# The sum of a unit's logits issued one place later on VectorE, in a delta-rule attention and mixture-of-experts kernel

## The chip, the cores and the metric

One core of a Trainium2 chip runs the whole program. The metric is the device time of one execution in microseconds, from three runs of the kernel; the profile is one further execution, with its own time.

## The reference

Four sequences of 768 tokens with eight heads of 48 features go through a delta rule; the 3072 rows of 384 that come out of it go through a layer of eight experts, each row to the one expert with the largest logit.

```python
k_n = k / (np.linalg.norm(k, axis=-1, keepdims=True) + 1e-06)
for t in range(S):
    y[:, :, t] = q_t @ state
    state = state + beta_t * outer(k_t, v_t - state @ k_t)
...
logits = x @ w_gate
expert_idx = np.argmax(logits, axis=1)
gate_w = softmax(logits)[expert_idx]
out[mask_e] = gate_w * (np.maximum(x[mask_e] @ w1[e], 0.0) @ w2[e])
```

## The kernel before

The work has two parts on one time line. The first part is attention: the 768 tokens are cut into six blocks of 128, and a **unit** n is one block of one of the four sequences (24 units). A main loop runs steps t = 0 to 26. In step t, TensorE computes `residual(t)` (products of states and earlier results, into the tile `ks`, lines L424 and L436), VectorE subtracts them from the values (`v_all`, L443), TensorE applies the inverse of a small triangular system (`apply`, L451, which reads `v_all`), and ScalarE copies the result to `u` (L455). The output of a unit follows three steps behind (`finish`): products of its query with the state (`yp`, L474), an update of the state (`ku`, L483, added on VectorE at L487), products with `u` (again `yp`, L492), two ScalarE copies to `yt` (L496). One step later `emit_x` multiplies `yt` with a selection matrix `esel` that also holds the gate's weights: four products (`xp`, L516) give the unit's 384 features and, in four pieces, its eight logits. ScalarE copies the features to `row` (L517), and VectorE sums the pieces of the logits to `rl` (TENSOR_REDUCE, L518).

The inverses of later blocks are computed on VectorE alone, as long chains of small operations on `lw`, `lg` and `tmp` (L384, L388). Nothing schedules them but the code: `beside(t, i)`, at seven places i of each step, issues a share of them (`inverses`), then a few pieces of the routing of finished rows (the list `fine`), and near the end shares of the second part. All engines work in the order of issue (a manual schedule), so the order of these calls is the order on each engine.

Routing of a pair of units (`pool_slots`, units 0 to 15) starts with a maximum on VectorE (`mx`, L617) and goes on with some twenty small operations on GpSimd (POOL in the rows): a mask of the chosen expert `oh_all` (L620 to L635), a count by four tiny products on TensorE (`pp`, L639 and L642), a ScalarE copy (`ct`, L645), positions (L647 to L654), the row numbers `sli` (L660), and two indirect DMAs that scatter the pair's rows to the experts' table `xg` in DRAM (L666). Each `yield` in these generators is a point where `beside` may go on with something else. For the later units `emit_slots` does the same on VectorE (L534 to L582, products at L552 and L555, scatters at L589); the last four units go through it one at a time. When the rows of units 16 and 17 have been scattered, `load_main` loads the first 256 rows of expert 0 (`xr`, L731), and TensorE transposes them (`xt`, L784), to begin with expert 0 while attention still runs (`early`, steps 23 to 26: first layer tiles h_0 to h_7 at L759, relu on ScalarE and VectorE at L762 and L763, weights split in two at L694 and L695).

Short PSUM tiles come from a ring of three buffers with the tag "y": `yp`, `ku`, `xp` and `pp` take them in the order of issue, and each waits until the last reader of the tile three places before it is done. GpSimd also copies a block's norms (`nt_all`, L339, four copies) when VectorE has transposed them (`r`, L334), masks the query products (`pm`, L277), and clears `lw` (L283).

The second part, from 302 us on, is the eight experts' layers on TensorE (`ffn`, products at L759 and L770).

Of the kernel before, what the change touches and what calls it, by code (L numbers as in the profile page):

```python
# [41 lines left out]
def deltanet_moe(ctx, tc, kt_d, qt_d, kn_d, v_d, beta_d, w_gate, w1, w2, out):  # L42
# [402 lines left out]
    def apply(t):  # L445

        ks, vn = tiles["ks", t], vt[t]
        for h in range(H):
            for q, n in stage(t):
                r = slice(32 * q, 32 * q + 32)  # L450
                nc.tensor.matmul(ks[r, h, :], lhsT=tiles[n // B]["wt"][r, n % B * H + h, :], rhs=vn[r, h, :],  # L451
                                 start=True, stop=True, tile_position=(32 * q, 32 * q), skip_group_check=True)
        for i, (q, n) in enumerate(reversed(stage(t))):
            r = slice(32 * q, 32 * q + 32)
            nc.scalar.copy(out=uview(n)[r], in_=ks[r])  # L455
            if i == 2:
                yield

    def finish(n):

        tb, b = n // B, n % B
        last = tb == NT - 1
        st, u = st_t[b], uview(n)
        qt, pm = qt_t[n % QTL], pm_t[n % QSL]
        yp = [pss.tile([128, NP // 2, C], F32, name=f"yp{tb}_{b}_0", tag="y", bufs=YB),
              psg_[-1].tile([128, NP // 2, C], F32, name=f"yp{tb}_{b}_1", tag="g")]

        def place(h, m):
            o = 64 * ((h // 2 + h) % 2)
            return yp[h // 2 % 2][o:o + m, h // 4, :]  # L470

        for h in range(H):
            r = slice(64 * (h % 2), 64 * (h % 2) + 64)
            nc.tensor.matmul(place(h, 64), lhsT=st[r, h // 2, r], rhs=qt[r, h // 2, :], start=(h < 4), stop=True,  # L474
                             tile_position=(r.start, 64 * ((h // 2 + h) % 2)), skip_group_check=True)
        yield
        if not last:
            ku = pss.tile([112, NP, D], F32, name=f"ku{tb}_{b}", tag="y", bufs=YB)
            for h in range(H):

                m = 64 if h % 2 == 0 else D
                kn = tiles[tb][b]["kn"].rearrange("t h d -> t (h d)")[:, h * D:h * D + m]
                nc.tensor.matmul(ku[64 * (h % 2):64 * (h % 2) + m, h // 2, :], lhsT=kn, rhs=u[:, h, :],  # L483
                                 start=True, stop=True, skip_group_check=True)
            for a in range(2):
                r = slice(64 * a, 64 * a + D)
                nc.vector.tensor_tensor(out=st[r, :, r], in0=st[r, :, r], in1=ku[r], op=ALU.add)  # L487
            if n + NB_ < NN - B:
                load_ku(n + NB_)
        yield  # L490
        for h in range(H):
            nc.tensor.matmul(place(h, D), lhsT=u[:, h, :], rhs=pm[:, h, :],  # L492
                             start=False, stop=True, skip_group_check=True)
        yt = lp.tile([128, NP, C], F32, name=f"yt{tb}_{b}", tag="yt", bufs=2)
        for o in range(2):
            nc.scalar.copy(out=yt[:, o::2], in_=yp[o])  # L496
        yield
        w = 1 if n >= NN - W1 else 2
        if n % w == 0:
            tiles["row", n // w, w] = (rp if n < NN - 2 else xq_[0]).tile([128, 2 if n < NN - 2 else 1, ROW], F32, name=f"row{tb}_{b}", tag="row", bufs=2)  # L500
            tiles["rl", n // w, w] = lp.tile([128, 2, E], F32, name=f"rl{tb}_{b}", tag="rl", bufs=2)
        row, rl = tiles["row", n // w, w], tiles["rl", n // w, w]
        row, rl = row[:, 0:w], rl[:, 0:w]
        emit_x(n, yt, row[:, n % w], rl[:, n % w])
        if n % w == w - 1:
            fine.append((pool_slots if n < PG else emit_slots)(tb, b - w + 1, w, row, rl))

# [1 line left out]
        t = st_t[b][:, p, :]  # L509
        return bass.AP(tensor=t.tensor, offset=t.offset, ap=[list(t.ap[0]), [64, 2], [1, D]])  # L510

    def emit_x(n, yt, row, rl):

        xp = pss.tile([128, NP, 2 * D + E], F32, name=f"xp{n // B}_{n % B}", tag="y", bufs=YB)
        for p in range(NP):
            nc.tensor.matmul(xp[:, p, :], lhsT=yt[:, p, :], rhs=esel[:, p, :], start=True, stop=True)  # L516
        nc.scalar.copy(out=row[:, 0:DM].rearrange("t (p c) -> t p c", p=NP), in_=xp[:, :, 0:2 * D])  # L517
        nc.vector.tensor_reduce(out=rl, in_=xp[:, :, 2 * D:].rearrange("t p e -> t e p"), axis=AX.X, op=ALU.add)  # L518

    def emit_slots(tb, b, w, row, rl):  # L520

# [454 lines left out]
    def beside(t, i):  # L976

        place[0] = 7 * t + i
        for tb in ROOT:
            if place[0] == ROOT[tb][0]:  # L980
                squares(tb)
            if place[0] == ROOT[tb][1]:
                root(tb)
        inverses((SPEND0 if t < B else SPEND if t < 3 * B else SPEND2)[i], t)
        for _ in range(STEPS[i] if t < NN - B else 4):
            if fine and not run(fine[0]):
                fine.pop(0)
        for _ in range(WSL.count((t, i))):
            run(W)
        for _ in range(ES.count((t, i))):  # L990
            ahead_step()

    fin = iter(())
    for t in range(NN + LAG):
        if t < NN and t % B == 0 and t > 0:
            while line and line[0].tb <= t // B:
                inverse_step(t)
            if t == NN - B:
                ep_.close()
                wq.append(ep.enter_context(tc.tile_pool(name="wr", bufs=1, side="right")))  # L1000
                xq_.append(ep.enter_context(tc.tile_pool(name="xq", bufs=1, side="right")))
                W = pieces()
                run(W)
        residual(t)
        beside(t, 0)
        chunk(ks_, t)
        run(fin)
        if t + 1 < NN + LAG and not B <= t < NN - B:
            scale_v(t + 1)
        if t + 1 < NN:  # L1010
            clear_u(t + 1)
        beside(t, 1)
        copies = apply(t)
        run(copies)
        for tb in range(1, NT):
            for i in range(NB):
                if t == B * (tb - 1) + i:
                    load_v(tb, i)
        fin = finish(t - LAG) if t >= LAG else iter(())
        run(fin)  # L1020
        beside(t, 2)
        run(fin)
        run(copies)

        if B <= t < NN - B:
            scale_v(t + 1, act=True)
        beside(t, 3)
        beside(t, 4)
        run(fin)
        beside(t, 5)  # L1030
        chunk(qs_, t)
        beside(t, 6)
        if t >= LAG:
            load_k(t - LAG + KTL)
            load_q(t - LAG + QTL)
        for x in slots[CL[t]:CL[t + 1]] if t + 1 < len(CL) else ():
            nc.sync.dma_start(out=x, in_=zrow[0:x.shape[0]].unsqueeze(1).broadcast_to(x.shape))
    i = 0
    run(fin)
    while fine:  # L1040
        if not run(fine[0]):
            fine.pop(0)
# [304 lines left out]
```

## Time and profile before

| | |
|---|---|
| median of 3 runs | 526.48 us (524.97 to 529.17) |
| profiled execution, its own time | 525.89 us |
| its span, first to last instruction | 524.2 us |
| TensorE, VectorE, ScalarE, GpSimd busy in the span | 463.6, 331.6, 269.5, 142.9 us |
| granted TensorE clock, mean | 0.955 |

Every number in a row of the trace is of the one profiled execution. Its time of 525.89 us is 1.7 us more than its span. A bracket at the end of a timeline row, such as [2.00 <-ACT row L517], is the time that the engine stood idle before that instruction, and what ended it. PE is TensorE's products, DVE is VectorE, ACT is ScalarE, POOL is GpSimd, SP issues most DMAs.

### The profile page before, as it was taken

Reading aid. Unit: us, or ns where it says so; the run is one execution under the profiler, and the core shown is the slowest. Engines: PE = TensorE matmul, PEld = TensorE weight load, DVE = VectorE, ACT = ScalarE, POOL = GpSimd, SP = SyncE. Lnnn points to the kernel's source line nnn. Section 1 sums busy time; section 2 is a strip of 40 time slices with the busy share of each in tenths; the row PEclk is TensorE's granted clock in tenths of the full one; section 3 lists DMA queues with packets and bytes.
Section 4 is the critical chain, followed back from the end, with each engine's and each line's share of the span. In section 5 each row is a group of like instructions: output and inputs, shape, how many; then the busy total and the mean of one; then the engine's idle time right before and its main releaser. Section 6 shows DMA issues by size and latency. Waiting matters only on the chain. (4 is left out here: it accounts for less than half of the span.)

```text
span 524.2 us, 17557 instructions
## 1 busy us (share of the span) xinstructions
PE 463.6 (88%) x7212; PEld 426.7 (81%) x7212; DVE 331.6 (63%) x996; ACT 269.5 (51%) x622; POOL 142.9 (27%) x305
## 2 busy tenths in 40 slices
PE   6866769899888888988789999999999999999995
PEld 4755658788776767777689889999999999999995
DVE  3989999698897689435654386636372827445330
ACT  2542236588676667755644246535354636354320
POOL 7002011465763655433130201020202020110202
PEclk9976689899999899898999999999999999999998
DMA  5878769569479557394442156555373636453001
GB/s 165 194 256 227 232 153 315 168 157 294 119 198 275 183 159 225 123 301 123 151 157 80 67 158 221 177 168 160 123 226 114 211 129 210 137 163 108 33 3 44
DMA packets 66060, 87.88 MB, mean 168 GB/s; under 512 B 26425, under 2 KB 50767, under 8 KB 65968
## 3 DMA queue, kind: packets, MB, share of 16 engines
q1 hardware_dynamic: 62512, 77.01, 50.2%
q0 software_dynamic: 3456, 9.57, 5.0%
q8 instruction: 67, 1.10, 0.9%
q14 instruction: 25, 0.20, 0.1%
HBM read 60.24 MB, written 23.56 MB: 160 GB/s over the span
## 5 line engine op out<-in xcount | busy, mean ns | idle before, releaser
L770 PE MATMUL y<-w2h,hx 128*128 128x384 f32 x352 | 93.8, 341 | 0.4 <-PEq L1143 0.4
L773 POOL DMA_INDIRECT out_dram<-yo,idx x32 | 30.7, 958 | 202.3 <-ACT yo L1116 129.8
L695 DVE TENSOR_TENSOR w2l<-w2r,w2h 128x768 fp32r<-128x768 f32 x32 | 31.2, 978 | 69.9 <-ACT w2h L694 69.7
L388 DVE TENSOR_TENSOR lw<-lw,tmp 128x84 f32<-128x84 f32 (+29 forms) x239 | 67.3, 316 | 0.4
L384 DVE TENSOR_TENSOR tmp<-lg,lw 128x84 f32<-128x84 f32 (+29 forms) x239 | 65.2, 307 | 2.5
L770 PEld LDWEIGHTS y<-w2h,hx 128*128 128x128 f32 x352 | 64.1, 188 | 0.7 <-issue 0.7
L455 ACT COPY u<-ks 32x384 f32<-32x384 f32 x96 | 45.1, 470 | 32.8 <-PE ks L451 30.3
L770 PE MATMUL y<-w2l,hx 128*128 128x384 f32 x176 | 59.4, 337 | 0.0
L759 PE MATMUL h<-xl,w1h 128*128 128x384 f32 (+1 forms) x168 | 57.5, 342 | 0.2 <-DVE xl L695 0.2
L759 PE MATMUL h<-xh,w1h 128*128 128x384 f32 (+1 forms) x168 | 57.5, 342 | 0.0
L759 PE MATMUL h<-xh,w1l 128*128 128x384 f32 (+1 forms) x168 | 57.4, 342 | 0.0
L762 ACT ACTIVATE hx<-h 128x448 fp32r<-128x448 f32 (+1 forms) x64 | 32.9, 518 | 33.1 <-PE h L759 32.3
L424 PE MATMUL ks<-st,kt 128*32 128x96 f32 x768 | 46.2, 257 | 2.4 <-issue 2.4
L1116 ACT ACTIVATE yo<-y,gt 128x384 f32<-128x384 f32 x21 | 12.2, 582 | 66.9 <-PE y L770 51.0
L763 DVE SCALAR_TENSOR_TENSOR hx<-h,hx 128x448 fp32r<-128x448 f32 (+1 forms) x64 | 36.9, 587 | 15.1 <-ACT hx L762 14.9
L277 POOL TENSOR_SCALAR_AFFINE_SELECT pm<-pm 128x1024 f32<-128x1024 f32 x24 | 26.6, 1110 | 71.2 <-ACT pm L276 68.6
L451 PE MATMUL ks<-v_all,wt 32*32 32x48 f32 x1536 | 25.7, 206 | 21.6 <-DVE v_all L443 18.9
L249 ACT COPY gg<-pg 128x512 f32<-128x512 f32 x48 | 25.8, 588 | 35.2 <-PE pg L266 35.2
L451 PEld LDWEIGHTS ks<-v_all,wt 32*32 32x32 f32 x1536 | 21.5, 107 | 26.0 <-DVE v_all L443 21.7
L424 PEld LDWEIGHTS ks<-st,kt 128*32 128x32 f32 x768 | 34.5, 113 | 5.8 <-issue 2.9
L266 PE MATMUL pq<-qt,kt 64*128 64x128 f32 x384 | 32.1, 299 | 2.3 <-issue 1.0
L695 DVE TENSOR_TENSOR w1l<-w1r,w1h 128x1024 fp32r<-128x1024 f32 x24 | 29.4, 1225 | 6.8 <-ACT w1h L694 6.8
(194 smaller groups left out, 987.9 us busy)
## 6 DMA issues: line engine op xcount, KB each, us to landing
w1r<-in_w_dram SPq DMA_DIRECT2D x24, 512.0 KB, 4.0
w2r<-in_w_dram SPq DMA_DIRECT2D x32, 384.0 KB, 3.7
kt<-in_kt_dram SPq DMA_DIRECT2D x24, 256.0 KB, 2.8
qt<-in_qt_dram SPq DMA_DIRECT2D x24, 256.0 KB, 5.8
xg<-zrow SPq DMA_DIRECT2D x7, 788.0 KB, 6.2
kg<-in_kt_dram SPq DMA_DIRECT2D x17, 256.0 KB
xr<-xg SPq DMA_DIRECT2D x7, 591.0 KB, 5.2
xn<-row SPq DMA_DIRECT2D x10, 394.0 KB, 5.1
```

The costliest lines, as they stand in the source:

```text
L266: nc.tensor.matmul(pg[a][:, p], lhsT=kt[r, p], rhs=xt[r, p], start=True, stop=True, tile_position=(64 * a, 0), skip_group_check=True)
L384: nc.vector.tensor_tensor(out=x, in0=lg[:, r0:r1, c:c + 1].broadcast_to([128, r1 - r0, b - a]), in1=lw[:, c:c + 1, a:b].broadcast_to([128, ...
L388: nc.vector.tensor_tensor(out=lw[:, r0:r1, a:b], in0=lw[:, r0:r1, a:b], in1=x, op=ALU.add)
L424: nc.tensor.matmul(ks[32 * q:32 * q + 32, 2 * p:2 * p + 2, :], lhsT=kt_t[n % KTL][:, p, 32 * q:32 * q + 32], rhs=st_view(n % B, p), start= ...
L451: nc.tensor.matmul(ks[r, h, :], lhsT=tiles[n // B]["wt"][r, n % B * H + h, :], rhs=vn[r, h, :], start=True, stop=True, tile_position=(32 * ...
L455: nc.scalar.copy(out=uview(n)[r], in_=ks[r])
L695: nc.vector.tensor_tensor(out=lo, in0=src, in1=hi.bitcast(F32), op=ALU.subtract)
L759: nc.tensor.matmul(ps, lhsT=w[:, d, fs], rhs=x_[:, d], start=(n == 0), stop=(n == len(terms) - 1))
L762: nc.scalar.activation(out=hh, in_=ps, func=AF.Relu)
L763: nc.vector.scalar_tensor_tensor(out=hl, in0=ps, scalar=0.0, in1=hh.bitcast(F32), op0=ALU.max, op1=ALU.subtract)
L770: nc.tensor.matmul(ps, lhsT=h(f)[h_], rhs=w2[w][:, f, :], start=(n == 0), stop=(n == len(terms) - 1))
L773: nc.gpsimd.indirect_dma_start(out=out, out_offset=bass.IndirectOffsetOnAxis(ap=idx, axis=0), in_=yo, in_offset=None, bounds_check=N - 1, ...
```

## The change

`emit_x` no longer sums the logits; it returns the PSUM tile `xp`. `finish` yields after it, and sums behind that yield. In step t the main loop now runs `finish` once more, behind `beside(t, 1)`: there the sum is issued, and there the unit pair's routing is added to the list `fine`. The four products and the ScalarE copy are issued where they were.

```diff
         row, rl = row[:, 0:w], rl[:, 0:w]
-        emit_x(n, yt, row[:, n % w], rl[:, n % w])
+        xp = emit_x(n, yt, row[:, n % w])
+        yield
+        nc.vector.tensor_reduce(out=rl[:, n % w], in_=xp[:, :, 2 * D:].rearrange("t p e -> t e p"), axis=AX.X, op=ALU.add)
         if n % w == w - 1:
             fine.append((pool_slots if n < PG else emit_slots)(tb, b - w + 1, w, row, rl))
...
-    def emit_x(n, yt, row, rl):
+    def emit_x(n, yt, row):
...
-        nc.vector.tensor_reduce(out=rl, in_=xp[:, :, 2 * D:].rearrange("t p e -> t e p"), axis=AX.X, op=ALU.add)
+        return xp
...
         beside(t, 1)
+        run(fin)
         copies = apply(t)
...
-    run(fin)
+    run(fin, 2)
```

Lines of the changed kernel are two higher behind the yield (L639 is L641 there), and the sum is at L506.

The order moves with it in three kinds of place. The first is TensorE in step 10, behind the last products of `residual` (`ks`): `pp` are the count products of the pair of units 4 and 5, `pg` and `xp` products of other units, L451 is `apply`. Before:

```order
L436 MATMUL ks_2505<-u_1750,gg_108 32x48
L639 LDWEIGHTS ltri
L639 MATMUL pp_0_2552<-oh_all,ltri 128x16
...
L266 MATMUL pg_3_1_2568<-kg_133 128x128
L516 MATMUL xp_2_2587<-esel,yt_2_2476 128x104 x4
L451 MATMUL ks_2505<-v_all,wt_1931 32x48 x3
```

Now:

```order
L266 MATMUL pg_3_0_2552<-kg_133 128x128
L266 MATMUL pg_3_1_2553<-kg_133 128x128
L518 MATMUL xp_2_2572<-esel,yt_2_2476 128x104 x4
L641 LDWEIGHTS ltri
L641 MATMUL pp_0_2584<-oh_all,ltri 128x16
...
L451 MATMUL ks_2505<-v_all,wt_1928 32x48 x3
```

The count products moved from the front of the group to directly ahead of `apply`. This is so in every second step from 6 to 20. On GpSimd, in step 9, two kinds of operation changed places; before:

```order
L660 CAST sli_2_2178<-sl_all 128x2
L666 DMA xg<-row_2_1741,sli_2_2178 3648x394
L339 COPY nt_all<-r_2041 32x32 x4
L277 AFFINE_SELECT pm_118<-pm_118 128x1024
L666 DMA xg<-row_2_1741,sli_2_2178 3648x394
```

Now:

```order
L662 CAST sli_2_2227<-sl_all 128x2
L339 COPY nt_all<-r_2033 32x32 x4
L668 DMA xg<-row_2_1726,sli_2_2227 3648x394
L277 AFFINE_SELECT pm_118<-pm_118 128x1024
L668 DMA xg<-row_2_1726,sli_2_2227 3648x394
```

The first scatter of units 2 and 3 moved behind the four copies of the norms. The second kind of place is VectorE around step 22, where `sli` are the row numbers of units 16 and 17, `w1l` a split of weights, and `v_all` the subtraction of step 22. Before:

```order
L574 TENSOR_REDUCE sl_all<-pos_0_4769 128x2
L582 CAST sli_0_4802<-sl_all 128x2
L695 TENSOR_TENSOR w1l_4612<-w1r_2_4468,w1h_4611 128x1024
L443 TENSOR_TENSOR v_all<-v_all,ks_4809 128x384
L518 TENSOR_REDUCE rl_2_4855<-xp_2_4856 128x8
```

Now:

```order
L576 TENSOR_REDUCE sl_all<-pos_0_4780 128x2
L697 TENSOR_TENSOR w1l_4609<-w1r_2_4468,w1h_4608 128x1024
L443 TENSOR_TENSOR v_all<-v_all,ks_4806 128x384
L584 CAST sli_0_4848<-sl_all 128x2
L407 TENSOR_TENSOR v_all<-v_all,nt_all 128x384
L506 TENSOR_REDUCE rl_2_4852<-xp_2_4853 128x8
```

The row numbers, which the scatters wait for, moved behind the weight split and the subtraction. The third is VectorE in step 25, where `he` are relu results of expert 0's tiles h_4 and h_5, and `oh_all` and `pos` belong to the routing of unit 21. Before:

```order
L763 SCALAR_TENSOR_TENSOR he_5353<-h_4_5354,he_5353 128x256
L548 TENSOR_TENSOR oh_all<-oh_1_5349,m_1_5351 128x8
L558 TENSOR_TENSOR pos_1_5398<-base,pp_1_5395 128x8
L763 SCALAR_TENSOR_TENSOR he_5353<-h_5_5401,he_5353 128x256
```

Now:

```order
L765 SCALAR_TENSOR_TENSOR he_5344<-h_5_5394,he_5344 128x256
L550 TENSOR_TENSOR oh_all<-oh_1_5390,m_1_5392 128x8
L560 TENSOR_TENSOR pos_1_5410<-base,pp_1_5407 128x8
```

The mask `oh_all` moved behind the relu of h_5; on TensorE the count products that read it moved behind the products of h_5.

## Rows read from the trace of the kernel before

**Rows 1.** Stretches: length; busy PE, PEld, DVE, ACT, POOL; clock; DMA share, rate.
```profile
85.76:217.59 131.83, 115.50 (x3360) 99.93 (x3359) 104.90 (x375) 93.91 (x284) 70.31 (x174) 0.96 0.70 201
...
301.70:505.00 203.30, 200.71 (x1183) 198.63 (x1184) 110.25 (x195) 99.00 (x168) 25.69 (x32) 1.00 0.48 151
```

**Rows 2.** TensorE's waits, 85 to 305 us: total us, times, longest.
```profile
PE ks L451 <- DVE v_all L443: 6.0, 9, 1.4
PE pp L639 <- POOL oh_all L635: 4.5, 3, 2.1
```

**Rows 3.** VectorE's waits, 85 to 230 us: total us, times, longest.
```profile
DVE rl L518 <- ACT row L517: 12.5, 8, 2.6
```

**Rows 4.** TensorE's timeline: step 10, one row of step 14, then of step 15.
```profile
139.44 0.17 PE L639 MATMUL pp<-oh_all,ltri 128*128 128x16 bf16 x1 [2.06 <-POOL oh_all L635]
...
139.61 1.16 PE L266 MATMUL pg<-kg 64*128 64x128 f32 x16
140.71 1.14 PE L516 MATMUL xp<-esel,yt 128*128 128x104 f32 x8
...
174.94 0.17 PE L639 MATMUL pp<-oh_all,ltri 128*128 128x16 bf16 x1 [2.04 <-POOL oh_all L635]
...
185.02 0.89 PE L451 MATMUL ks<-v_all,wt 32*32 32x48 f32 x64 [0.64 <-DVE v_all L443]
```

**Rows 5.** GpSimd's timeline, steps 8 to 10.
```profile
125.41 1.09 POOL L666 DMA_INDIRECT xg<-row,sli  x1 [0.34 <-POOL sli L660]
128.01 0.28 POOL L339 COPY nt_all<-r 32x32 f32<-32x32 f32 x1 [1.51 <-DVE r L334]
132.66 1.01 POOL L339 COPY nt_all<-r 32x32 f32<-32x32 f32 x3 [4.36 <-DMA xg<-row,sli]
...
136.05 0.23 POOL L620 TENSOR_TENSOR row<-rl,mx 128x16 f32<-128x16 f32 x1
```

**Rows 6.** GpSimd's timeline, steps 12 to 14: the scatters, and the copies behind them.
```profile
159.83 1.11 POOL L666 DMA_INDIRECT xg<-row,sli  x1 [0.61 <-POOL sli L660]
...
167.01 0.99 POOL L666 DMA_INDIRECT xg<-row,sli  x1 [1.94 <-DMA xg<-row,sli]
...
170.93 0.94 POOL L339 COPY nt_all<-r 32x32 f32<-32x32 f32 x3 [1.65 <-DMA xg<-row,sli]
```

**Rows 7.** VectorE's timeline: the sum of step 9, and one row of step 16.
```profile
132.25 0.19 DVE L518 TENSOR_REDUCE rl<-xp 128x8 f32<-128x32 f32 x1 [2.00 <-ACT row L517]
...
195.63 0.53 DVE L384 TENSOR_TENSOR tmp<-lg,lw 128x192 f32<-128x192 f32 x2
```

**Rows 8.** VectorE's timeline, steps 21 and 22.
```profile
242.99 0.17 DVE L582 CAST sli<-sl_all 128x2 int32<-128x2 f32 x1
244.50 1.25 DVE L695 TENSOR_TENSOR w1l<-w1r,w1h 128x1024 fp32r<-128x1024 f32 x1 [1.34 <-ACT w1h L694]
245.68 0.54 DVE L443 TENSOR_TENSOR v_all<-v_all,ks 128x384 f32<-128x384 f32 x1
```

**Rows 9.** GpSimd's timeline, steps 21 and 22: a mask, then a scatter.
```profile
243.59 1.09 POOL L277 TENSOR_SCALAR_AFFINE_SELECT pm<-pm 128x1024 f32<-128x1024 f32 x1 [5.88 <-ACT pm L276]
244.84 1.78 POOL L589 DMA_INDIRECT xg<-row,sli  x1 [0.16 <-issue]
```

**Rows 10.** TensorE's timeline: one row each of steps 16, 23, 24, 25.
```profile
195.61 0.61 PE L483 MATMUL ku<-u,ku 128*64 128x48 f32 x15
...
257.40 0.41 PE L784 MATMUL xt<-ident,xr 128*128 128x128 f32 x2 [1.45 <-DMA xr<-xg]
...
269.51 0.17 PE L552 MATMUL pp<-oh_all,ltri 128*128 128x8 bf16 x1 [1.00 <-DVE oh_all L548]
...
278.28 0.17 PE L552 MATMUL pp<-oh_all,ltri 128*128 128x8 bf16 x1
```

**Rows 11.** The stretch behind the wait of step 14: columns as in rows 1.
```profile
176.60:180.00 3.40, 3.40 (x79) 2.95 (x69) 2.25 (x10) 2.76 (x9) 2.31 (x8) 0.50 0.03 9
```

**Rows 12.** All uses of the table `xg`: from a DMA's issue to its landing.
```profile
DMA to landing us min/median/max: 2.7/4.9/7.2
```

## The prediction

> **What bounds the kernel now.** I read the busy times by stretch first, then the waits by engine, then timelines of the steps where the waits lie. The stretches say where time can be won at all: in the experts' part TensorE is busy 200.7 of 203.3 us, so whatever happens before it only moves its start, one for one [rows 1]. In attention's middle TensorE is busy 115.5 of 131.8 us (88%) and VectorE 104.9 (80%) [rows 1]. Neither is full, so the step is a chain that goes through several engines, and the waits on TensorE are what a step can lose.
>
> Those waits are few. Between 85 and 305 us TensorE stands 6.0 us ahead of `apply` for the subtraction, nine times, and 4.5 us ahead of the count products for GpSimd's mask, three times [rows 2]. VectorE stands much longer just ahead of the sum that is moved: 12.5 us in eight steps, always for ScalarE's copy of the same `xp` tile [rows 3]; in step 9 it is 2.00 us [rows 7]. That is what the change fills with inverses. But time that VectorE gets back counts only where the next subtraction was late because of it, and all that TensorE loses to late subtractions is the 6.0 us.
>
> **What the change does, part by part.** It adds and removes no instruction. One sum per unit (24 of them) moves behind one share of inverses, two to four small operations. With it everything moves that is issued from the list `fine`: the routing of a pair begins one place later, and each later piece of it shifts by a place, on VectorE, GpSimd, ScalarE, TensorE and on SP's queue.
>
> *Waits of the subtraction.* In step 14 VectorE's idle time before the sum is followed by a late subtraction in step 15, and TensorE waits 0.64 us for it [rows 4]. I take 0.6 us as won. The bounds are 0 and all 6.0 us [rows 2]; I stay near the lower one, since most of the nine waits lie in steps where VectorE had no idle time before the sum, and simply was not done with the inverses.
>
> *Count products, steps 8 and 10.* In step 10 TensorE waited 2.06 us and then did `pg` and `xp`, from 139.61 to 141.77, before `apply` [rows 4]. Now these 2.16 us of products stand ahead of the count, so its turn comes at 139.44 - 2.06 + 2.16 = 139.5, when the mask was just ready: the wait is hidden, 2.06 us won, if the mask is not later. GpSimd's order moved there too. Its first scatter, at 125.41, now stands behind four copies that can begin at 128.01 and take 1.3 us, so it goes out at 129.4; in return the copies no longer stand 4.36 us for its landing [rows 5]. The second scatter needs that landing, 4.9 us in the median and 7.2 at most [rows 12], and takes 1.1 us: routing then begins at 135.4 to 137.7, against 136.05 [rows 5]. So the mask is 0.7 us earlier to 1.7 us later, and between 0.5 and 2.06 us are won; I take 2.06, because the median landing gives it. Step 8 has the remainder of the 4.5 us, 4.5 - 2.06 - 2.04 = 0.4 us, under the same cover: 0.4 won (0 to 0.4).
>
> *Count products, step 14.* Here the 2.04 us [rows 4] should not go away. There is no `pg` any more in these steps, only `xp` (1.14 us) goes ahead. And the mask hangs on a chain that began at the count products of step 12: positions, a scatter at 159.83, its landing, the second scatter at 167.01, its landing, the copies at 170.93 [rows 6], and then the mask. The count of step 12 itself moves behind `xp`, 1.14 us, and its copy on ScalarE behind the copy of a row, so the chain starts 1.1 to 1.3 us later. What the cover gives, the chain takes: I count 0.2 us lost, between 1.1 won and 0.6 lost.
>
> [...]
>
> *The rows of units 16 and 17.* This is the place where the change costs. The row numbers were made at 242.99; now they come behind a split of weights, which itself waits for ScalarE, and behind the subtraction, which ends at 245.68 + 0.54 = 246.22 [rows 8]: 3.2 us later. GpSimd's scatter was held by a mask until 244.68 and started at 244.84 [rows 9]. Now it can start at 246.22 + 0.17 + 0.34 (the lag behind the numbers in rows 5) = 246.7, 1.9 us later. The second scatter waits for its landing, the load of expert 0's rows for the second, and TensorE for the load: it already stood 1.45 us there [rows 10]. So the whole 1.9 us is added to that wait. Bounds: 0.3 and 3.2 us; the lower if the scatter, 1.78 us long there, takes 1.0 as it does elsewhere [rows 6, 9] and the landing is short.
>
> *Routing of unit 21, step 25.* The mask now stands behind the relu of h_5 on VectorE, and the count behind the products of h_5. Step 24 shows what that costs: the count stood 1.00 us for a mask behind the relu of the tile that had just been computed; in step 25 it stood for nothing [rows 10]. I count 0.9 us lost (0 to 1.0). Step 24 keeps its wait: its pair moves by one tile together.
>
> *The rest.* The unit's sum is done later, so `xp` is free later; that is a rival below. Scatters of the last units come later as well, but their rows are read only by the experts' part; their cover is some twenty microseconds of expert 0's tiles, and I cost them at nothing (1 us if it is gone).
>
> **The sum.** Won: 0.6 + 2.06 + 0.4 = 3.1 us. Lost: 0.2 + 1.9 + 0.9 = 3.0 us. Net 0.1 us faster: 525.89 becomes 525.8. The profiled execution lies 0.6 us below the median of the runs, 526.48, so I carry the difference over to the median: 526.4 us.
>
> **Rivals.**
>
> *VectorE is the bound of attention's middle.* Then all 12.5 us [rows 3] come back: 526.5 - 12.5 = 514 us. For it: VectorE is behind the subtraction in nine steps [rows 2]. Against it: it is busy only 80% [rows 1], and the subtraction of a step cannot be earlier than its products.
>
> [...]
>
> [...]
>
> *The state products wait for the moved sum (slower).* In the ring of three, `ku` follows the unit's `xp` by three places in every second step from 6 to 20, now that `pp` stands between them. In step 16 the sum would come behind an operation that ends at 195.63 + 0.53 = 196.16 [rows 7], while `ku` started at 195.61 [rows 10]: 0.55 us of waiting, in eight steps 4.4 us, 530.8. Against it: in steps where VectorE stood idle before the sum it is not later at all, and in step 16 VectorE itself is what the next step waits for.
>
> **How the numbers follow.** The forecast, gains and losses that cancel, has a chance of 0.52, and by itself lies between 524 and 529. The bound of VectorE 0.03, GpSimd's waits 0.17, the late rows 0.18, the state products 0.10. A measurement of this kernel can tell about 1% (5.3 us) from no change. Faster by more needs less than 521.2: all of the first rival and half of the second, 0.12. Slower by more needs over 531.7: the slower two at their upper ends together, 0.12. Within 1%: 0.76. The range that leaves out 2 in 10 goes from 521.5 to 531.
>
> **What would show it right or wrong.** Right: the wait of VectorE before the sum falls from 12.5 us to a few; the count of step 10 stands for nothing and that of step 14 again about 2 us; the transposes of step 23 wait 3 us or more; a wait of some 0.9 us appears before the count of step 25; the experts' part keeps its 203 us. Wrong: the subtraction's 6.0 us fall by more than half, `ku` shows waits for the sum, or the transposes wait no longer than before.

## The result and the profile after

The changed kernel takes 529.11 us in the median of 22 runs (526.11 to 535.71), the kernel before on the same chip 527.32 (521.54 to 533.77, 22 runs). The ratio is 1.0082, with a 95% interval of 1.0057 to 1.0107: slower by 0.8%, some 4.3 us. (The ratio leaves disturbed runs out; over all runs the means differ by 2.7 us.) Compared once more it is 1.0058 (1.0016 to 1.0100). The forecast was 526.4 us, no change, within a range of 521.5 to 531.

The profiled execution of the changed kernel has a span of 533.8 us, longer than its typical run. A second profile of the same kernel has 519.6 us, and a second one of the kernel before 532.8 instead of 524.2. So one pair of profiles says little about a difference of 4 us; below, sums are means over profiles, and rows are read for what stands where.

The stretches of the changed kernel, in the columns of [rows 1]:

```profile
87.96:222.08 134.12, 119.87 (x3363) 102.79 (x3363) 100.85 (x376) 94.46 (x285) 69.70 (x173) 0.95 0.66 190
222.08:310.80 88.72, 76.60 (x1520) 66.73 (x1519) 41.27 (x135) 43.08 (x102) 23.94 (x38) 0.96 0.43 141
310.80:514.00 203.20, 200.56 (x1181) 198.31 (x1182) 110.42 (x197) 98.49 (x167) 26.05 (x33) 1.00 0.48 151
```

The experts' part keeps its length (203.20 us, 203.30 before). All that changed is ahead of it: attention's middle is 134.1 instead of 131.8 us, and the part between them 88.7 instead of 84.1 (301.70 - 217.59).

TensorE's waits, 85 to 315 us, in the columns of [rows 2]:

```profile
PE ks L451 <- DVE v_all L443: 3.5, 5, 1.9
PE pq L266 <- issue: 3.1, 2, 2.7
PE pp L641 <- POOL oh_all L637: 2.6, 1, 2.6
...
PE yp L492 <- issue: 2.4, 1, 2.4
...
PE pp L554 <- DVE oh_all L550: 2.2, 3, 1.0
...
PE xt L786 <- DMA xr<-xg: 0.9, 1, 0.9
```

VectorE's waits, 85 to 235 us:

```profile
DVE st L487 <- PE ku L483: 16.9, 13, 4.6
DVE v_all L443 <- ACT pm L276: 9.3, 7, 3.0
DVE v_all L443 <- PE ks L436: 6.8, 2, 4.1
DVE rl L506 <- ACT row L519: 2.7, 4, 1.5
```

The wait ahead of the sum is nearly gone, 12.5 us [rows 3] to 2.7. In its place VectorE stands for TensorE's products `ku`: 16.9 us, against 8.0 in the kernel before. On TensorE the waits for the subtraction are 3.5 us instead of 6.0 and those for the mask 2.6 instead of 4.5 [rows 2]; rows that end in "issue" now stand among the largest. How much of this belongs to the change and how much to the one execution is taken up below.

TensorE's timeline of the changed kernel: step 10, one row of step 14, then steps 23, 24 and 25.

```profile
143.90 1.43 PE L266 MATMUL pg<-kg 64*128 64x128 f32 x16
145.26 1.14 PE L518 MATMUL xp<-esel,yt 128*128 128x104 f32 x8
146.23 0.17 PE L641 MATMUL pp<-oh_all,ltri 128*128 128x16 bf16 x1
...
180.14 0.17 PE L641 MATMUL pp<-oh_all,ltri 128*128 128x16 bf16 x1 [2.64 <-POOL oh_all L637]
...
264.82 0.63 PE L786 MATMUL xt<-ident,xr 128*128 128x128 f32 x4 [0.93 <-DMA xr<-xg]
...
278.98 0.17 PE L554 MATMUL pp<-oh_all,ltri 128*128 128x8 bf16 x1 [1.00 <-DVE oh_all L550]
...
288.72 0.17 PE L554 MATMUL pp<-oh_all,ltri 128*128 128x8 bf16 x1 [1.00 <-DVE oh_all L550]
```

Against [rows 4, 10]: the count of step 10 has no bracket any more (2.06 us before), that of step 14 keeps its wait (2.04, now 2.64), the count of step 25 has a new one (none, now 1.00), and the transposes, for which the prediction wanted 3 us or more, stand for 0.93.

GpSimd, steps 9 and 10 of the changed kernel:

```profile
131.31 1.23 POOL L339 COPY nt_all<-r 32x32 f32<-32x32 f32 x4
132.84 1.11 POOL L668 DMA_INDIRECT xg<-row,sli  x1 [0.29 <-POOL nt_all L339]
135.03 1.09 POOL L277 TENSOR_SCALAR_AFFINE_SELECT pm<-pm 128x1024 f32<-128x1024 f32 x1 [1.09 <-ACT pm L276]
136.81 1.21 POOL L668 DMA_INDIRECT xg<-row,sli  x1 [0.69 <-DMA xg<-row,sli]
...
142.62 0.43 POOL L637 TENSOR_SCALAR oh_all<-oh 128x16 bf16<-128x16 f32 x1
```

The four copies no longer stand 4.36 us for a landing [rows 5], and the mask of step 10 was there at 143.05, 3.2 us before TensorE came to the count at 146.23.

### The profile page after: what moved, and what is told of

Its sections match the earlier page's. It is cut to its first block, busy times and chain, and to the rows that moved or that the text cites. A ratio compares the mean times of both kernels' runs of the same rounds, so it can differ in the third digit from the quotient of the medians.

```text
span 533.8 us, 17554 instructions
## 1 busy us (share of the span) xinstructions
PE 469.3 (88%) x7212; PEld 430.7 (81%) x7212; DVE 327.2 (61%) x996; ACT 270.1 (51%) x622; POOL 145.6 (27%) x305
## 5 line engine op out<-in xcount | busy, mean ns | idle before, releaser
L384 DVE TENSOR_TENSOR tmp<-lg,lw 128x84 f32<-128x84 f32 (+29 forms) x239 | 63.8, 301 | 2.6
L388 DVE TENSOR_TENSOR lw<-lw,tmp 128x84 f32<-128x84 f32 (+29 forms) x239 | 64.7, 304 | 0.4
L424 PE MATMUL ks<-st,kt 128*32 128x96 f32 x768 | 47.4, 263 | 2.3 <-issue 2.3
L277 POOL TENSOR_SCALAR_AFFINE_SELECT pm<-pm 128x1024 f32<-128x1024 f32 x24 | 29.8, 1242 | 70.8 <-ACT pm L276 70.7
L451 PE MATMUL ks<-v_all,wt 32*32 32x48 f32 x1536 | 28.7, 211 | 22.2 <-DVE v_all L443 19.2
L1119 ACT ACTIVATE yo<-y,gt 128x384 f32<-128x384 f32 x21 | 12.2, 582 | 67.4 <-PE y L772 51.5
L451 PEld LDWEIGHTS ks<-v_all,wt 32*32 32x32 f32 x1536 | 23.5, 111 | 26.4 <-DVE v_all L443 21.3
L266 PEld LDWEIGHTS pq<-qt,kt 64*128 64x128 f32 x384 | 26.8, 202 | 9.7 <-issue 5.2
```

Of the source, the lines that this page charges most:

```text
L266: nc.tensor.matmul(pg[a][:, p], lhsT=kt[r, p], rhs=xt[r, p], start=True, stop=True, tile_position=(64 * a, 0), skip_group_check=True)
L384: nc.vector.tensor_tensor(out=x, in0=lg[:, r0:r1, c:c + 1].broadcast_to([128, r1 - r0, b - a]), in1=lw[:, c:c + 1, a:b].broadcast_to([128, ...
L388: nc.vector.tensor_tensor(out=lw[:, r0:r1, a:b], in0=lw[:, r0:r1, a:b], in1=x, op=ALU.add)
L424: nc.tensor.matmul(ks[32 * q:32 * q + 32, 2 * p:2 * p + 2, :], lhsT=kt_t[n % KTL][:, p, 32 * q:32 * q + 32], rhs=st_view(n % B, p), start= ...
```

## The experiments

One line decides most of them: where the generator yields before the sum, or between the sum and the list `fine`. The ratio is to the kernel before on the same chip. "Tail" is the time in that kernel's profile from the first `apply` product of step 20 to the first product of the experts' part.

| run | what is moved | ratio (95%) | tail, us |
|---|---|---|---|
| changed kernel | all | 1.0082 (1.0057 to 1.0107) | 79.7 |
| e12 | all, once more | 1.0058 (1.0016 to 1.0100) | 78.9 |
| e1 | units 0 to 15 | 1.0037 (1.0001 to 1.0072) | 74.3 |
| e16 | units 0 to 15, once more | 1.0023 (0.9992 to 1.0055) | 73.8 |
| e2 | units 16 to 23 | 1.0049 (1.0012 to 1.0085) | 81.2 |
| e7 | units 16 to 19 | 1.0065 (1.0014 to 1.0117) | 83.4 |
| e8 | units 20 to 23 | 0.9986 (0.9951 to 1.0020) | 77.8 |
| e3 | sums of units 0, 2 to 18, no routing | 1.0047 (1.0014 to 1.0080) | 74.7 |
| e9 | all sums, no routing | 1.0010 (0.9973 to 1.0047) | 76.4 |
| e4 | routing alone | 1.0126 (1.0089 to 1.0164) | 80.3 |
| e13 | all, row numbers of 16 and 17 put back | 1.0027 (0.9984 to 1.0071) | 78.0 |
| e11 | nothing (kernel before) | 1.0007 (0.9969 to 1.0044) | 76.5 |
| e5 | nothing, 64 products added | 0.9990 (0.9956 to 1.0024) | 74.4 |
| e10 | all sums, 64 added | 0.9994 (0.9958 to 1.0031) | 74.2 |
| e15 | units 0 to 15, 64 added | 0.9986 (0.9926 to 1.0047) | 73.9 |
| e6 | all, 64 added | 1.0043 (1.0007 to 1.0079) | 76.6 |
| e14 | as e13, 64 added | 1.0058 (1.0027 to 1.0088) | 78.9 |

The tail of the kernel before is 75.2 us in its first profile. e11 shows how far to trust the third digit: the kernel before against itself comes out at 1.0007, with an interval of 0.4% to either side.

**Which units: e1, e2, e3, e16.** In e1 and e16 only the early units yield, in e2 only the late ones, in e3 only the first of each pair, whose sum releases no routing:

```diff
-        yield
+        if n < PG:
+            yield
```

(e2: `n >= PG`; e3: `n % w != w - 1`.)

> Only units 0 to 15 sum and route one place later; units 16 to 23 stand as in the kernel before. If the loss lies in attention's end (the routing of units 16 to 23, theory A), this is within 0.3% of the kernel before, or 0.3 to 0.6% faster, since the three waits on GpSimd's mask lie here. If it lies in attention's middle (theory B: the state products, or the count products directly ahead of apply, now hold TensorE), it is 0.5 to 1% slower, as the whole change is.

> Only units 16 to 23 sum and route one place later; units 0 to 15 stand as in the kernel before. Theory A: 0.6 to 1% slower (3 to 5 us), with longer waits before the transposes of step 23, before apply in steps 22 to 24 and before the counts of steps 24 and 25. Theory B: no more than 0.2% (1 us) slower.

> The sum is moved only for the first unit of each pair (units 0, 2, to 18); no routing moves, since that starts at the pair's second unit. If the move of the sum costs anything by itself (the state products wait for it, theory B), this is 0.3 to 0.5% slower; if only the routing that follows it costs (theory A), it is within 0.2%, or up to 0.3% faster where VectorE's wait before the sum goes.

> Only units 0 to 15 moved, once more. Theory A and rival J both expect 1.001 to 1.005 of the kernel before here, as in the first run (1.0037); below 0.998 would say that the first run misled. The count of step 10 stands for nothing in its profile, and that of step 14 for 1.5 to 3.5 us.

The early units alone give no gain (1.0037, 1.0023), where the prediction's terms for them add up to 3.1 us won, 0.6%; the 0.37% lies between what theory A (at most 0.3% slower) and theory B (0.5 to 1%) gave. The late units alone cost, with 0.49% a little under the 0.6 to 1% that theory A gave. The two halves, 0.37% and 0.49%, add up to the whole change, 0.82%, within intervals of 0.4% to either side. e3 was slower by 0.5%, the number that theory B gave for a cost of the sum itself, with a profile like that of the kernel before (tail 74.7). e9, which moves all the sums, has no such cost, so I take no mechanism from e3; what made it slower stays open. In e16 the count of step 14 stood for 5.41 us, outside the 1.5 to 3.5 expected.

**Sum or routing: e4, e9, e10.** In e4 the sum stays and the yield stands behind it. In e9 the sum goes behind the inverses, but ahead of the routing's pieces of the same place, so that the routing keeps its places; e10 adds the 64 products of e5.

```diff
         inverses((SPEND0 if t < B else SPEND if t < 3 * B else SPEND2)[i], t)
+        if i == 1:
+            run(fin)
...
         beside(t, 1)
-        run(fin)
```

> The sum stays at the old place, and only the routing of a finished pair or unit begins one place later. If the routing costs (theory A), this is as slow as the whole change, 0.6 to 1%; if the sum's own place costs (theory B), it is within 0.3%.

> Only the 24 sums are issued behind the share of inverses; the pieces of the routing keep the places that they have in the kernel before, so TensorE, ScalarE, GpSimd and SP have its order, and on VectorE the sum alone has moved. Theory E (the moved sum is worth something, and what the change loses is the later routing): VectorE's wait ahead of the sum falls from 12.5 us to under 4, the count of step 10 still waits about 2 us, from the products of step 20 to the experts' part it is 74 to 76 us as before, and the time is 0.2 to 0.6% below the kernel before. Rival F (the time that VectorE gets back is worth nothing, since it then stands for the products ku or the next residual): its wait for ku grows from 8 us by about as much as the wait ahead of the sum falls, and the time is within 0.2% of the kernel before. Rival G (the sum itself, standing later, holds the ring of three and costs): 0.3 to 0.6% above.

> The sum alone moved, and the 64 small products added at the start, which shift the ends of the instruction blocks on TensorE. Against the shifted kernel before (0.999 of the kernel before): theory E expects 0.993 to 0.997 of the kernel before, rival F 0.997 to 1.001, rival G 1.002 or more. If only one of this and the unshifted one is faster, what is gained is where the blocks end and not the sum.

The routing alone costs 1.3%, more than the whole change, though the two intervals overlap. The sum alone is worth nothing within 0.4% (1.0010; against the shifted kernel before, 0.9994 to 0.9990). VectorE's waits of e9, 85 to 230 us:

```profile
DVE st L487 <- PE ku L483: 13.6, 13, 1.9
...
DVE rl L506 <- ACT row L519: 6.5, 5, 2.6
```

Ahead of the sum it wins 6.0 us (12.5 to 6.5), ahead of `ku` it loses 5.6 (8.0 to 13.6). VectorE is early and then waits for TensorE. That is rival F, and the time agrees with it. The rows alone would not show it, since e5, which moves no sum, has the same two waits at the same sizes:

```profile
DVE st L487 <- PE ku L483: 12.2, 10, 3.3
...
DVE rl L518 <- ACT row L517: 6.3, 8, 1.6
```

One expectation for e9 failed: its order on TensorE is that of the kernel before, so the count of step 10 was to wait about 2 us, and it stood for nothing. So that wait, the largest term of the prediction's gain, is there in some executions and not in others. The kernel before once more (e11), then e7 and e9, none of which moves the routing of the early units:

```profile
143.50 0.17 PE L639 MATMUL pp<-oh_all,ltri 128*128 128x16 bf16 x1 [1.83 <-POOL oh_all L635]
...
139.99 0.17 PE L642 MATMUL pp<-oh_all,ltri 128*128 128x16 bf16 x1 [2.06 <-POOL oh_all L638]
...
139.81 0.18 PE L641 MATMUL pp<-oh_all,ltri 128*128 128x16 bf16 x1
```

**The tail: e7, e8, e13, e14.** e7 yields only for units 16 to 19, e8 only for units from 20 on. e13 is the whole change with more pieces of the routing in step 21, which brings the row numbers of units 16 and 17 back ahead of the weight split and the subtraction; e14 is e13 with the 64 products.

```diff
-        for _ in range(STEPS[i] if t < NN - B else 4):
+        for _ in range((STEPS[i] if t < NN - B else 4) + (4 if (t, i) == (21, 2) else 0)):
```

> Only the sums, and with them the routing, of units 16 to 19 are issued one place later; all others stand as before. Theory C (the late rows of units 16 and 17 are most of what the routing of the last units costs): from the products of step 20 to the first product of the experts' part 78 to 80 us, against 75.2 before and 81.2 with all of units 16 to 23 moved; the excess lies in steps 20 to 23, step 25 keeps its 13.0 us; time 0.5 to 0.8% above the kernel before. Rival D (it is the single units 20 to 23): 75 to 76 us there, and no measurable difference in time.

> Only the sums, and with them the routing, of units 20 to 23 are issued one place later. Theory C (only the count of step 25 waits, about 1.0 us for the mask of unit 21): step 25 takes 14.0 us instead of 13.0, from the products of step 20 to the experts' part 76.2 us against 75.2 before; time 0.2% above the kernel before. Rival D (the single units carry the cost of 4.5 to 6 us): 79 to 81 us there and a time 0.8 to 1.1% above.

> The whole change, but in step 21 four more pieces of the routing are issued behind the third share of inverses, so that the row numbers of units 16 and 17 stand ahead of the weight split and of the subtraction of step 22 again, as in the kernel before; all else stays late. Theory C (the late rows of this pair cost 2.0 us and mostly also a stretch at half the clock): from the subtraction of step 22 to the transposes 10.9 to 12.2 us as before, not 13.5 or more; step 25 keeps its 14.05 us; from the products of step 20 to the experts' part 75.5 to 77.5 us; time 0.1 to 0.3% above the kernel before (0.6 to 0.8% with the change). Rival H (it is the late routing as a whole): 78 us or more there, and 0.5 to 0.8% above.

> The repaired change with the 64 small products added at the start, which shift the instruction blocks on TensorE by half of one. Theory C: below the changed kernel with the same shift (1.0043) by 0.2 to 0.6%, so 0.998 to 1.002 of the kernel before. Rival H: 1.003 to 1.006.

e8 has the count's wait of step 25 and no measurable cost in time (0.9986); its tail of 77.8 us lies between what theory C (76.2) and rival D (79 to 81) gave:

```profile
288.10 0.17 PE L555 MATMUL pp<-oh_all,ltri 128*128 128x8 bf16 x1 [1.01 <-DVE oh_all L551]
```

e7 has the late rows at their worst, with a tail of 83.4 us, above the 80 that theory C allowed. Its timeline of TensorE at the transposes:

```profile
261.50 0.66 PE L787 MATMUL xt<-ident,xr 128*128 128x128 f32 x2 [4.00 <-DMA xr<-xg]
```

and the stretch around and behind that wait, with the clock in the third column from the end:

```profile
260.80:271.04 10.24, 9.54 (x118) 8.17 (x118) 4.80 (x14) 4.55 (x10) 1.09 (x1) 0.50 0.43 145
```

With the wait of 4 us come 10.24 us at a granted clock of 0.50, 9.54 of them for the 118 products from the transposes on. In the kernel before, the 118 products from its transposes on take 6.20 us at a clock of 1.00:

```profile
257.40:263.60 6.20, 5.64 (x118) 4.72 (x119) 3.30 (x11) 4.34 (x10) 1.11 (x2) 1.00 0.65 202
```

So by estimate 3.3 us more are lost. In the changed kernel itself the same delay is seen in other rows. VectorE, steps 21 and 22:

```profile
250.16 1.22 DVE L697 TENSOR_TENSOR w1l<-w1r,w1h 128x1024 fp32r<-128x1024 f32 x1
251.29 0.55 DVE L443 TENSOR_TENSOR v_all<-v_all,ks 128x384 f32<-128x384 f32 x1
251.76 0.16 DVE L584 CAST sli<-sl_all 128x2 int32<-128x2 f32 x1
```

GpSimd, the two scatters of these rows:

```profile
252.20 1.04 POOL L591 DMA_INDIRECT xg<-row,sli  x1 [2.68 <-DVE sli L584]
258.72 0.98 POOL L591 DMA_INDIRECT xg<-row,sli  x1 [5.48 <-DMA xg<-row,sli]
```

The scatter starts 0.91 us behind the start of the subtraction; in [rows 8, 9] it started 0.84 us ahead of it. From the start of that subtraction to the transposes it is 11.5 us in the mean of the nine profiles in which no late unit's routing is late (10.9 to 12.2: the kernel before, e1, e3, e5, e9, e10, e11, e15, e16) and 13.4 us in the mean of the five with all late units late (11.5 to 14.2: the changed kernel, e2, e4, e6, e12). The mean hides two cases: four of the five have 13.5 to 14.2 us, and e6 has 11.5, no more than without the change. In all five the first scatter starts 0.9 us behind the subtraction and takes 1.0 or 1.1 us. Its landing makes the difference: 4.5 us behind the issue in e6, 6.0 to 6.2 in e2, e4 and e12, 5.0 to 5.6 in the kernels that are not late, as far as their traces tell the landing. With the row numbers put back it is 12.0 in e13 and 11.5 in e14, and GpSimd's two scatters of e13 stand as in the kernel before:

```profile
246.36 1.72 POOL L591 DMA_INDIRECT xg<-row,sli  x1 [1.21 <-DVE sli L584]
251.99 1.29 POOL L591 DMA_INDIRECT xg<-row,sli  x1 [3.91 <-DMA xg<-row,sli]
```

So theory C holds for the term, 1.9 us in the mean. It does not hold for the whole tail: e13 and e14 still need 78.0 and 78.9 us there, above the 77.5 that C allowed, as rival H had it (78 or more). Their times are 0.3%, at the upper end that C gave, and 0.6%, which is H's; they do not separate from those of the change (0.8%, 0.6%; shifted 0.4%). Putting the rows back is no cure that I could measure.

**What the "issue" waits are: e5, e6, e11, e12, e15.** In all these profiles TensorE's waits for "issue" of more than half a microsecond, between 85 and 312 us, lie 127 products apart, or a multiple of that, within three (but for one of 0.58 us in e13). The DMA queue "instruction" of the page moves 67 packets of 16,384 bytes in the kernel before and in the changed one, and one lands 1.1 to 1.7 us before each of these waits ends. To test that they are blocks of instructions that come late, 64 small products whose result nobody uses were added at the start, half of 127:

```diff
             nc.tensor.matmul(wm, lhsT=busy[:, 0:128], rhs=busy, start=True, stop=True)
+        for _ in range(64 if k == 5 else 0):
+            nc.tensor.matmul(wm[:, 0:16], lhsT=busy[:, 0:128], rhs=busy[:, 0:16], start=True, stop=True)
```

> The kernel before with 64 small products (16 columns each, result unused) added behind the first five at the very start, where TensorE soon waits for the first load; nothing else is changed. They push every later instruction of TensorE by half of the 127 products that lie between two of its waits for 'issue'. Theory A (those waits are instruction blocks that come late; where a block ends near a wait for another engine, it costs 1 to 2.7 us, elsewhere nothing): the waits for 'issue' stay at the same counts of products from the program's start (1235, 1362, ... 2124, ... 4791), and so fall on other operations; their sum between 85 and 312 us is anything from 6 to 18 us (10.5 before), and the time differs from the kernel before by up to 4 us, to either side. Theory B (the waits belong to the operations at which they stand, or cost nothing): they stay at the same operations, and the time is that of the kernel before plus 0 to 0.8 us for the added products.

> The changed kernel with the same 64 small products added at the start. Theory A (half or more of what the change costs is where the instruction blocks end, by chance): the waits for 'issue' between 85 and 312 us move to other operations, and their sum differs from the 15.7 us of the changed kernel by 4 us or more; against the shifted kernel before, the time differs by something else than the 0.8% of the unshifted pair: between -0.4% and +0.5%, or over 1.3%. Theory B (what the change costs is in the order of the routing of units 16 to 23, wherever blocks end): the shifted pair differs by 0.6 to 1.1%, as the unshifted one, and from step 20 to the first product of the experts' part the shifted changed kernel needs 4 to 6 us more than the shifted kernel before.

> Only units 0 to 15 moved (the sum and the routing on GpSimd), with the 64 small products at the start. Theory A (the gain of some 2 to 3 us is there, and the place of the instruction blocks took it back in the unshifted run): 0.5% below the shifted kernel before, so 0.992 to 0.996 of the kernel before. Rival J (the later routing of the early units gives nothing back, wherever the blocks lie): 0.998 to 1.003.

> The kernel before itself, as one of the kernels that are compared. Its ratio should be within 0.2% of 1; what it is off shows how far a difference of a few tenths of a per cent can be trusted. Its profile shows what of the middle part differs between two executions of one kernel: theory A (waits for instruction blocks and stretches at the lower clock vary from execution to execution) expects steps 4 to 20 to differ from the 139.7 us of the first profile by 2 us or more, theory B (each step has its fixed length) by less than 0.5 us.

> The changed kernel once more. Time 0.5 to 1.1% above the kernel before. From the products of step 20 to the first product of the experts' part 78 to 81 us (79.7 in its first profile, 75.2 in the kernel before): the subtraction of step 22 to the transposes some 13.5 us instead of 11.7, step 25 at 14.05 us, and one more stretch at a granted clock of 0.50 than before. If it is under 76.5 us, the late rows are not the cause.

The kernel before, from the start of the span up to such a wait (the number behind PE busy counts its products):

```profile
0.00:230.92 230.92, 188.02 (x4791) 161.54 (x4791) 183.99 (x673) 135.48 (x376) 96.51 (x254) 0.91 0.72 205
```

and its timeline of TensorE there:

```profile
230.93 0.49 PE L266 MATMUL pq<-qt,kt 64*128 64x128 f32 x4 [1.02 <-issue]
```

The same two views of e5:

```profile
0.00:225.40 225.40, 180.32 (x4791) 155.73 (x4792) 182.11 (x670) 131.70 (x369) 99.84 (x251) 0.92 0.73 208
```

```profile
225.54 0.28 PE L451 MATMUL ks<-v_all,wt 32*32 32x48 f32 x6 [2.17 <-issue]
```

The wait stayed behind the 4791st product and fell on another operation: theory A. What the runs show is the fixed count, and the packet that lands shortly before; that the packets are the blocks is my reading. What one such place costs differs: behind that count it is 1.02 us in the kernel before and 1.92 in e11, the same kernel; 2.73 us in the changed kernel and 1.58 in e12. The largest is in e6, in the middle of `apply`:

```profile
204.85 0.39 PE L451 MATMUL ks<-v_all,wt 32*32 32x48 f32 x9 [4.17 <-issue]
```

The loss seems to survive the shift: e6 over e5 is 1.0043 / 0.9990 = 1.0053, by some 0.5% to either side, below the 0.6 to 1.1% that theory B gave and above theory A's 0.5%. The tail of e6 is 2.2 us longer than that of e5, where theory B wanted 4 to 6. So the pair decides little between them. Theory A for e15, that the early units' gain of 0.5% would show with other block ends, is not borne out (0.9986 against 0.9990 without them), but the interval of e15, 0.9926 to 1.0047, does not shut it out. e11's steps 4 to 20, counted from products to products, took 145.3 us where the first profile had 139.7, the same kernel. e12 took 78.9 us in the tail, as expected, with TensorE's waits, 85 to 300 us:

```profile
PE ks L451 <- DVE v_all L443: 5.1, 6, 2.1
...
PE pp L554 <- DVE oh_all L550: 2.2, 3, 1.0
...
PE pp L641 <- POOL oh_all L637: 0.4, 2, 0.3
```

The waits of the middle, between the subtractions of steps 4 and 20, as means over profiles without added products:

| | profiles | length, us | for other engines and DMAs | "issue" | half of the time at a clock of 0.50 |
|---|---|---|---|---|---|
| early units not moved (before, e2, e7, e8, e11) | 5 | 140.3 (136.6 to 144.9) | 10.2 | 6.9 | 5.4 |
| early units moved (changed, e1, e12, e13, e16) | 5 | 138.9 (129.0 to 148.7) | 6.8 | 8.6 | 4.4 |

With the 64 products the one profile of e5 has 3.4, 12.1 and 1.7 us in 136.5, and the mean of e6, e14 and e15 is 3.3, 14.4 and 9.6 us in 146.0.

Two things hide in the means. The waits for other engines and DMAs are 3.4 and 2.1 us in the two profiles of the changed kernel, but 8.4 in e1, 10.0 in e16 and 10.0 in e13, whose middle has the order of the changed kernel; the kernels that do not move the early units have 8.1 to 13.7. And of the "issue" waits only 7.0 and 7.3 us stand at the counts that lie 127 products apart; the other 1.4 us of the second row are waits of up to 0.58 us at other counts, in the changed kernel, e13 and e16, for which no row tells a cause.

## Why the prediction was right and wrong

**VectorE is not the bound: right.** Of its 12.5 us most came back, nothing of it shows in the time, and e9 shows the sum alone to be worth nothing within 0.4%. The 0.6 us for the subtraction of step 15 are not seen: with the early units alone moved, TensorE still waits there for 0.70 us (e1) and 0.92 us (e16), and its waits for the subtraction up to 315 us sum up to 7.1 and 6.4 us, against 6.0 and 6.5 in the two profiles of the kernel before.

```profile
182.38 1.06 PE L451 MATMUL ks<-v_all,wt 32*32 32x48 f32 x64 [0.70 <-DVE v_all L443]
...
194.23 1.00 PE L451 MATMUL ks<-v_all,wt 32*32 32x48 f32 x48 [0.92 <-DVE v_all L443]
```

**Count products: right in the place, wrong in the price.** The waits of steps 8 and 10 are gone in all six profiles, without added products, that move the routing of the early units; step 14's is not: 2.64 us, and 0.2 to 5.4 in other profiles of either kind, as the prediction had it. But 2.06 us was the price of one execution: of the seven profiles, without added products, that leave this routing where it was, three have some 2 us of waiting in step 10 (2.06, 1.83 and 2.06), e3 has 0.23, the other three have none, and the mean is 0.88. The landing was misread as well, at no harm to the term: [rows 12] mix the scatters with the table's clears and loads, and the list of DMA issues of the kernel before has its 24 scatters alone, with 4.2 us in the median at the end of the line, where the prediction used 4.9.

```profile
xg<-row,sli POOLq DMA_INDIRECT x24, 4.2
```

That GpSimd's waits would go altogether was rightly held unlikely (0.17).

**Rows of units 16 and 17: right in size, wrong in the sign to look for.** 1.9 us were forecast; the scatter starts 1.75 us later against the subtraction, and from the subtraction to the transposes it is 1.9 us more in the mean, 2.0 to 2.6 in four profiles and nothing in e6. That is the forecast's lower bound, which it tied to a short scatter and a short landing; the agreement of the mean is partly luck. In the changed kernel the time does not show as a longer wait of the transposes, since TensorE itself came there later. The stretch from the products of step 22 to the transposes, in the columns of [rows 1], in the changed kernel and then in the kernel before:

```profile
251.90:264.82 12.92, 10.70 (x297) 8.94 (x297) 5.99 (x15) 7.04 (x15) 3.11 (x3) 0.87 0.50 145
246.28:257.40 11.12, 8.82 (x296) 7.36 (x297) 6.09 (x15) 6.93 (x15) 2.80 (x3) 1.00 0.51 144
```

At a mean granted clock of 0.87 TensorE was busy for 10.70 us with what took 8.82 us before. A bracket measures the last in a chain only; the distance between two fixed operations would have been the sign.

**Unit 21, step 25: right.** 1.00 us of waiting; the step takes 14.05 us in every kernel in which the routing of units 20 to 23 is late (the changed one, e2, e4, e6, e8, e12, e13, e14) and 12.8 to 13.0 in every other: 1.07 us, where 0.9 were forecast.

**The step that failed: "Won: 0.6 + 2.06 + 0.4 = 3.1 us".** It took waits of one execution that go away in attention's middle for time that goes away. The early units alone make the kernel no faster: 1.0037, 1.0023, and 0.9986 against 0.9990. The rows show in its place that the 0.6 us of step 15 stay, that the 2.06 us of step 10 are 0.88 in the mean, and that with the early units alone moved TensorE's waits for other engines and DMAs in the middle still sum up to 8.4 and 10.0 us, where the kernels that do not move them have 10.2 in the mean. That is 1.0 us less in the mean, and far less than the spread: this part differs by 6 to 13 us between two profiles of one kernel (139.3 and 144.9 us for the kernel before, 142.0 and 129.0 for the changed one, 135.8 and 148.7 for the early units alone). What takes back the last part of the gain stays open. By my reading a block of instructions that comes late could do it, if it was covered as long as TensorE stood for a mask, and is bared when that wait goes. But the waits at block ends are hardly longer with the early units moved (7.3 us against 7.0), so the rows do not bear this out, and no run took the late blocks away.

One of the waits 127 products apart took up to 4.17 us (e6). Their sum in the middle, 7.0 and 7.3 us in the means without added products, is of the size of all waits there for other engines and DMAs (10.2 and 6.8 us); with the 64 products it is 12 to 13 us, against 3.4 and 3.3.

**A second, smaller miss, perhaps: the tail.** Lost were to be 1.9 + 0.9 = 2.8 us there. The tail is 74.8 us in the mean of the nine profiles named above and 79.3 in the mean of the five, 4.5 us more: 1.9 for the rows, 1.07 for step 25, and 1.5 us for which no one row stands, in steps 20 to 22 and 23 to 24, where "issue" waits and stretches at a granted clock of 0.50 come and go. The changed kernel alone has 79.7, 78.9 and, with the 64 products, 76.6 us (e6), where the kernel before has 75.2, 76.5 and 74.4 (e5): 3.0 us more in the mean, close to what was forecast. The forecast's sum has no term for a stretch at a granted clock of 0.50 behind the late rows, such as the one that by estimate cost 3.3 us in e7. The 530.8 us of the state products would fit the ratio, but by chance, for no `ku` of either profile waits for the sum.

**The sum, put right.** Nothing measurable won in the middle in place of 3.1 us, and 3.0 to 4.5 lost in the tail in place of 2.8: some 3 to 4.5 us slower than before, against 4.3 by the ratio and 2.7 by the means. That the two signs would cancel was the forecast; the loss was there, the gain was not.

## What to carry to other kernels

Price one by one what a change delays; both delays priced here came out near their price. A wait that it removes is another matter: read it from several profiles before it is called a gain, since it may be there in some executions only, and ask whether the next thing on that engine is ready: here "issue" waits at fixed counts of products took 7.0 us of the middle with the early units where they were and 7.3 us with them moved. When work released by an operation is queued behind it (here the whole routing behind one sum of 0.2 us), move the operation without its followers first: here that was worth nothing, and the followers were the cost. Before a difference of a few microseconds is read from two profiles, take a second profile of the same kernel.

## What the runs showed of the hardware

Between 85 and 312 us TensorE stood at counts of products that lie 127 or a multiple apart, within three, for up to 4.17 us (e6). 64 more products at the start moved the wait behind the 4791st product from `pq` (1.02 us, kernel before) to `apply` (2.17 us, e5), and not to another count. The wait at one count differs between executions of one kernel (1.02 and 1.92 us; 2.73 and 1.58). Stretches at a granted clock of 0.50 stand around or behind some of TensorE's waits: 3.4 us behind the wait of step 14 in the kernel before [rows 11], 6.83 us around the end of the 2.64 us of step 14 in the changed kernel, 10.24 us around the 4.00 us of e7.

```profile
179.47:186.30 6.83, 6.16 (x122) 5.33 (x123) 2.26 (x10) 4.39 (x15) 4.72 (x14) 0.50 0.23 70
```

The two profiles of the changed kernel have spans of 533.8 and 519.6 us; 13.0 of these 14.2 us lie between steps 4 and 20, where the first has 5.5 us more of "issue" waits and 10.2 us more at a granted clock of 0.50.
